# A real Fourier transform by matrix products: the second transform's features folded once more, into even and odd frequencies

## The chip, the cores and the metric

The kernel runs on one core of a Trainium2 chip. Its time is that of one execution on the device in microseconds. A core has five engines that take their own instructions in order and wait for each other by semaphores: TensorE (matrix products, with a weight load ahead of each), VectorE, ScalarE, GpSimd and SyncE; DMA queues move data beside them.

## The reference, cut to what matters

```python
# attention over 64-blocks (B=4, H=8, S=576, D=64), then x: (4, 576, 512)
x = x + relu(layernorm(x) * g_ln @ w_ch1) @ w_ch2            # first FFN, hidden 2048
X = np.fft.fft(x, axis=1)                                    # first transform: 576 tokens
X = np.fft.fft(X, axis=2)                                    # second transform: 512 features
u = x + np.real(X)
out = u + relu(layernorm(u) @ w2_ch1) @ w2_ch2               # second FFN
```

Only the real part of the two transforms is needed: cosines of tokens with cosines of features, less sines with sines.

## The kernel before, in words

The kernel goes through five stages that overlap: attention, first FFN, transform, second FFN and the preparation of weights for both. All products run on TensorE; precision beyond f16 is had by splitting each operand into a high and a low f16 part and adding three products (high-high, high-low, low-high), so each sum over 128 rows is three matmuls.

Tokens are kept in tiles by symmetry. For a batch b, X["E", b] holds 256 tokens and X["F", b] their mirror images; 64 tokens of each batch that are left over stand together in X["L"].

The transform of batch b has three steps.

- `dft_a1` (L1386) adds and subtracts E and F (xe, xo), which serves the token transform, and then `fold_rows` (L1337) adds feature f to feature 512 - f (for cosines over features) and subtracts it (for sines). The sums stand in places 1 to 255 and the differences in 257 to 511 of one row of 512, places 0 and 256 being features 0 and 256 themselves. Token 288 has a row of its own in one partition (g0). Then it scales by a power of two and splits into f16 parts: ge for the main tiles, gL for the left-over tokens, g0s for the one row; gL and g0s go by DMA from GpSimd's queue into a small tile gS.
- `dft_a2` (L1419) is the first matrix product (L1433), by features: five blocks (0, 1: cosines; 2, 3: sines; 4: the single feature 256), each with the token tables ct or sn, 289 columns. `dft_y` (L1438) copies and splits each result into y with ScalarE (L1440) and VectorE (L1441).
- `dft_b` (L1448) is the second matrix product, over features, from y: with the table cd (257 cosine columns, L1457; a single feature is added by two matmuls with the table row) and the table sd (255 sine columns, L1467). `dft_b_main` calls it for two row tiles of a batch, and once more without sines for the "pf" tile; `dft_b_left` calls it for the left-over tokens. `dft_apply` adds the result to E and F.

Beside this, `w_second` streams the second FFN's weights, in 32 pieces of one load each: ScalarE makes signs (L217), VectorE merges (L218), ScalarE squares and sums (L239). Pieces land in staging tiles (`w_stage`); the first 12 of them borrow buffers of the transform that are free until the transform starts, named by the list TAGS (L94) in rotation. The thirteenth and later ones use the two buffers wr.

What sets the order: `merge` gives each stream of work a planned time and takes the item with the earliest. A transform is six items of planned weight 10 (`dft_a1`), 1.2 each (`dft_a2`) and 2 (`dft_b_main`), between FFN products. Within this, instructions without a due partner may be placed ahead, by priority. TensorE then works strictly in that order.

Of the kernel before, what the change touches and what calls it, by code (L numbers as in the profile page):

```python
# [8 lines left out]
F32 = mybir.dt.float32  # L9
# [81 lines left out]
YE = 300  # L91
DV = (1, 0, 3)
R_F = 0.3
TAGS = ("wr", "wr", "xe", "xo", "ge", "y")  # L94
NT = 12
BLOCKS = ("B11", "B21", "B22", "T1", "T3", "T2", "T4")

# [2 lines left out]
def fused_kernel(ctx: ExitStack, tc: tile.TileContext, io: dict):  # L100
# [75 lines left out]
    def w_stage(n, name):  # L176
        shape = [128, n, 512, 4]
        if "pool" in wst:
            wst["k2"] = wst.get("k2", -1) + 1
            tag = TAGS[wst["k2"] % len(TAGS)] if wst["k2"] < NT else "wr"  # L180
            return wst["pool"].tile(shape, I16, tag=tag, bufs=WR if tag == "wr" else 1, name=name)
        wst["k"] = wst.get("k", -1) + 1
        if wst["k"] % 3 == 2 and wst["k"] < T3:
            return wpool.tile(shape, I16, tag="w", bufs=9, name=name)
        return a_tile(shape, I16, "stage", name)
# [1127 lines left out]
    def dft_setup(dctx):  # L1313
        wst["w1"] = ctx.enter_context(tc.tile_pool(name="w1pool", bufs=1))
        dp = dctx.enter_context(tc.tile_pool(name="dpool", bufs=1))
        D_["p"] = dp
        wst["pool"] = dp
        w_signs(dp, WN[1], NZ[1])
        for nm, shape in (
            ("ct", [128, 2, 2, 289]), ("sn", [128, 2, 2, 289]),  # L1320
            ("ctl", [98, 289]), ("snl", [96, 289]),
            ("cd", [128, 2, 2, 257]), ("sd", [128, 2, 2, 255]),
        ):
            t = dp.tile(shape, F16, name="c_" + nm)
            nc.gpsimd.dma_start(out=t, in_=io["c_" + nm])
            D_[nm] = t
        D_["row"] = dp.tile([128, 289], F16, name="c_row")
        nc.gpsimd.memset(D_["row"], 0.0)
        nc.gpsimd.dma_start(out=D_["row"][0:1, :], in_=io["c_row"])
        D_["yl"] = dp.tile([128, 4, 2, 128], F16, name="yl")  # L1330
        for nm, m, n in (("yl5", 2, 128), ("y5", 3, 289)):
            D_[nm] = dp.tile([128, m, n], F16, name=nm)
            nc.gpsimd.memset(D_[nm], 0.0)
        D_["invL"] = dp.tile([128, 1], F32, name="invL")
        D_["nL"] = dp.tile([128, 1], F32, name="nL")

    def fold_rows(a, d, out):  # L1337


        rev = slice(511, 256, -1)  # L1340
        nc.vector.tensor_tensor(
            out=out[..., 1:256], in0=a[..., 1:256], in1=a[..., rev], op=ALU.add
        )
        nc.vector.tensor_tensor(
            out=out[..., 257:512], in0=d[..., 1:256], in1=d[..., rev], op=ALU.subtract
        )

    def split(hi, lo, src, s):
        nc.scalar.activation(out=hi, in_=src, func=AF.Copy, scale=s)
# [11 lines left out]
    def dft_left_fold():  # L1361

        dp = D_["p"]
        xl = X["L"]
        sumsq(D_["nL"], [xl])
        xe, xo = (dp.tile([128, 2, DM], F32, tag=t, name=t) for t in ("xe", "xo"))
        a, d = xe[:, 0], xo[:, 0]
        nc.vector.tensor_tensor(out=a, in0=xl[:, 0], in1=xl[:, 1], op=ALU.add)
        nc.vector.tensor_tensor(out=d, in0=xl[:, 0], in1=xl[:, 1], op=ALU.subtract)
        fL = D_["fL"] = dp.tile([128, DM], F32, name="fL")  # L1370
        fold_rows(a, d, fL)
        nc.vector.tensor_copy(out=fL[:, 0:257:256], in_=a[:, 0:257:256])
        D_["gL"] = dp.tile([128, 2, DM], F16, name="gL")

    def dft_left_split(b, s):
        dp = D_["p"]
        q = slice(32 * b, 32 * b + 32)
        g = D_["gL"]
        split(g[q, 0], g[q, 1], D_["fL"][q], s[q, 0:1])
        st = dp.tile([98, DM], F16, tag="gS", bufs=GSB, name="gS")  # L1380
        nc.gpsimd.memset(st[96:98, 257:512], 0.0)
        for i, a in enumerate((0, 1, 0)):
            nc.gpsimd.dma_start(out=st[32 * i:32 * i + 32], in_=g[q, a])
        return st

    def dft_a1(b):  # L1386
        dp = D_["p"]
        E, F = X["E", b], X["F", b]
        n1 = sm.tile([128, 1], F32, tag="dn1", name="dn1")
        sumsq(n1, [E, F])  # L1390
        xe, xo = (dp.tile([128, 2, DM], F32, tag=t, name=t) for t in ("xe", "xo"))
        nc.vector.tensor_tensor(out=xe, in0=E, in1=F, op=ALU.add)
        nc.vector.tensor_tensor(out=xo, in0=E, in1=F, op=ALU.subtract)
        q = slice(32 * b, 32 * b + 32)
        nc.vector.tensor_tensor(out=n1[q], in0=n1[q], in1=D_["nL"][q], op=ALU.add)
        tot = all_sum(n1, 1, "dt")
        fold_rows(xe, xo, xe)
        r0, g0 = xo[0:1, 0], xo[0:1, 1, 0:257]
        nc.vector.tensor_tensor(
            out=g0[:, 1:256], in0=r0[:, 1:256], in1=r0[:, 511:256:-1], op=ALU.add  # L1400
        )
        nc.vector.tensor_copy(out=g0[:, 0:257:256], in_=r0[:, 0:257:256])
# [7 lines left out]
        g0s = dp.tile([1, 2, 257], F16, tag="g0s", name="g0s")  # L1410
        split(g0s[:, 0], g0s[:, 1], g0, s[0:1, 0:1])
        for a in range(2):
            nc.gpsimd.dma_start(out=st[96 + a:97 + a, 0:257], in_=g0s[:, a])
        g = dp.tile([128, 2, 2, DM], F16, tag="ge", name="ge")
        split(g[:, 0], g[:, 1], xe, s[:, 0:1])
        D_["g", b] = (g, st, s, inv)
        D_["y", b] = dp.tile([128, 4, 2, 289], F16, tag="y", name="y")

    def dft_a2(b, blk):  # L1419


        g, st, s, inv = D_["g", b]
        ev = blk in (0, 1, 4)
        f0, n = {0: (0, 128), 1: (128, 128), 2: (257, 128), 3: (385, 127), 4: (256, 128)}[blk]
# [20 lines left out]
        yl = D_["yl5"][0:1] if blk == 4 else D_["yl"][0:m, blk]  # L1445
        nc.gpsimd.tensor_copy(out=yl[:, :, 32 * b:32 * b + 32], in_=y[:, :, 256:288])

    def dft_b(yc, y5, ys, pool_bank):  # L1448

        mm = []  # L1450
        for a, w in ((0, 0), (0, 1), (1, 0)):
            for f in range(2):
                mm.append((yc(f, a), D_["cd"][:, f, w, :]))
        for a in range(2):
            mm.append((y5(a), D_["row"][:, 0:257]))
        for i, (l, r) in enumerate(mm):
            nc.tensor.matmul(  # L1457
                out=pool_bank[:, 0:257], lhsT=l, rhs=r, start=(i == 0), stop=(i == len(mm) - 1)
            )
        if ys is None:  # L1460
            return
        mm = []
        for a, w in ((0, 0), (0, 1), (1, 0)):
            mm.append((ys(0, a), D_["sd"][:, 0, w, :]))
            mm.append((ys(1, a), D_["sd"][0:127, 1, w, :]))
        for i, (l, r) in enumerate(mm):
            nc.tensor.matmul(  # L1467
                out=pool_bank[:, 257:512], lhsT=l, rhs=r, start=(i == 0), stop=(i == len(mm) - 1)
            )

    def dft_apply(pq, pf, inv, e, f):

# [207 lines left out]
def _hl(a):  # L1680
    a = np.asarray(a, np.float64) * CS
    hi = a.astype(np.float16)
    lo = (a - hi.astype(np.float64)).astype(np.float16)
    return np.stack([hi, lo])


def _consts():
# [13 lines left out]
    row = np.zeros((2, 289), np.float16)  # L1701
    row[:, 1::2] = CS
    c["ctl"] = np.concatenate([c["ctl"], row])
    f = np.arange(256)
    l = np.arange(257)
    cd = _hl(np.cos(2 * np.pi * ((f[:, None] * l[None, :]) % 512) / 512.0))
    c["cd"] = cd.reshape(2, 2, 128, 257).transpose(2, 1, 0, 3)
    f = np.arange(1, 257)
    l = np.arange(1, 256)
    sd = _hl(np.sin(2 * np.pi * ((f[:, None] * l[None, :]) % 512) / 512.0))  # L1710
    sd[:, 255] = 0
    c["sd"] = sd.reshape(2, 2, 128, 255).transpose(2, 1, 0, 3)
    row = np.zeros((1, 289), np.float16)
    row[0, 0:257] = CS * (1 - 2 * (np.arange(257) % 2))
# [65 lines left out]
```

## Time and profile before

| | |
|---|---|
| three runs | 994.78, 996.1, 999.83 us; median 996.1 |
| the profiled execution | 997.26 us, span 995.5 us |
| granted TensorE clock, mean over the span | 0.982 of full speed |
| TensorE busy | 946.1 us, 95% |
| VectorE busy | 673.7 us, 68% |
| ScalarE busy | 490.2 us, 49% |
| GpSimd busy | 72.5 us, 7% |

Busy times are sums over one profiled execution and an average over stages with different limits: a stage in which one engine is the limit can be one in which another is idle. The chain of waits is followed back from the last instruction, at each step to what released it. The ends of matmuls are modelled and overlap, so the pace of a series is read from their starts.

### The profile page before, as it was taken

The numbers are of one execution on the slowest core, as the hardware profiler recorded it, in microseconds if no ns is written. First come the engines' busy times: TensorE is split into PE (matmuls) and PEld (weight loads), VectorE is DVE, ScalarE is ACT, GpSimd is POOL, SyncE is SP. The second block draws the span as 40 slices with busy tenths as digits, with TensorE's granted clock in tenths as the row PEclk, the third lists the DMA queues.
The fourth block names the chain that finished last, engine by engine and source line by source line (L and its number), as shares of the span: only waits on it lengthen the run. The fifth ranks groups of instructions, "written<-read, shape, count | busy, mean of one in ns | idle before, by whom it ended". The sixth has DMA issues, their size and how long they took to land.

```text
span 995.5 us, 19447 instructions
## 1 busy us (share of the span) xinstructions
PE 946.1 (95%) x7758; PEld 700.8 (70%) x7758; DVE 673.7 (68%) x1677; ACT 490.2 (49%) x852; POOL 72.5 (7%) x184
## 2 busy tenths in 40 slices
PE   8898989998998999998999889999999999999998
PEld 6786654674674674766576665858588888888887
DVE  3886696665767666566587887669476776765754
ACT  5887664554554564426656654325153352342431
POOL 1000000002001010040011120100000000000000
PEclk9998999999999999999999989999999999999999
DMA  7657536758667666567408657011110111101100
GB/s 259 225 186 212 133 79 138 153 114 154 139 126 154 129 146 103 99 139 298 146 8 249 212 177 255 8 22 65 43 22 23 33 23 33 22 23 43 23 22 22
DMA packets 159195, 110.95 MB, mean 111 GB/s; under 512 B 134141, under 2 KB 141318, under 8 KB 157056
## 3 DMA queue, kind: packets, MB, share of 16 engines
q1 hardware_dynamic: 154640, 104.87, 40.8%
q0 software_dynamic: 2352, 4.32, 1.9%
q8 instruction: 61, 1.00, 0.4%
q10 hardware_dynamic: 2112, 0.52, 0.2%
q14 instruction: 30, 0.25, 0.1%
HBM read 64.19 MB, written 11.01 MB: 76 GB/s over the span
## 4 chain that ended last, share of the span: by engine, by line
PE 42%; DVE 7%; DMA 5%; ACT 3%; issue 1%; POOL 0%; ACTq 0%; POOLq 0%; DVEq 0%; SPq 0%
PE g L698 15%; PE s L748 13%; PE g L627 6%; PE g L679 4%; PE g L652 3%; DMA wr<-in_w 2%; DMA xnT1L<-xs 1%; ACT junk L239 1%; DVE ws L218 1%; DVE wq L339 1%; ACT sign L217 1%; DVE hT L637 1%; PE ya L1433 1%; DMA xnT2('F', 0)_7977<-xs 1%; DMA d<-ws 1%
## 5 line engine op out<-in xcount | busy, mean ns | idle before, releaser
L627 PEld LDWEIGHTS <-wq 128*128 128x128 f16 x2112 | 206.5, 99 | 47.9 <-issue 19.0
L652 PE MATMUL g<-wq,hT 128*128 128x512 f16 x768 | 184.2, 383 | 2.1 <-ACT hT L636 1.3
L698 PEld LDWEIGHTS <-wq 128*128 128x128 f16 x1344 | 131.5, 98 | 15.4
L652 PEld LDWEIGHTS <-hT 128*128 128x128 f16 x768 | 74.6, 99 | 90.2 <-issue 5.8
L748 PEld LDWEIGHTS <-hs 128*128 128x128 f16 x1176 | 115.1, 98 | 13.3
L715 ACT ACTIVATE hr<-g,tk 128x256 f32<-128x256 f32 x112 | 47.0, 470 | 143.1 <-PE g L698 143.1
L890 PE MATMUL pv<-vh,PT 128*128 128x65 f16 (+1 forms) x704 | 102.9, 203 | 14.6 <-DMA PT<-P 5.3
L919 DVE SCALAR_TENSOR_TENSOR P<-e,P 128x768 f16<-128x768 f32 (+2 forms) x56 | 54.6, 976 | 69.9 <-ACT P L918 69.8
L890 PEld LDWEIGHTS <-PT 128*128 128x128 f16 x1056 | 82.1, 101 | 28.1 <-issue 19.0
L723 DVE TENSOR_TENSOR hr<-hr 128x128 f32<-128x128 f32 x224 | 65.4, 292 | 48.3 <-ACT hr L715 40.4
L1167 ACT ACTIVATE e<-st,aq 128x384 f32<-128x384 f32 (+2 forms) x80 | 48.9, 652 | 91.3 <-DVE aq L1164 80.8
L748 PE MATMUL s<-tT,hs 128*128 128x256 f16 x672 | 75.7, 273 | 0.0
L637 DVE SCALAR_TENSOR_TENSOR hT<-g,hT 128x512 f16<-128x512 f32 x88 | 59.8, 683 | 19.3 <-ACT hT L636 19.1
L636 ACT ACTIVATE hT<-g 128x512 f16<-128x512 f32 x88 | 51.4, 588 | 34.2 <-PE g L627 34.1
L679 PE MATMUL g<-wq,hT 128*128 128x512 f16 x288 | 63.8, 379 | 0.2 <-DVE wq L339 0.2
L890 PE MATMUL pv<-vl,PT 128*128 128x64 f16 (+1 forms) x352 | 62.7, 203 | 0.0
L730 DVE TENSOR_TENSOR hs<-hr,hs 128x896 f16<-128x896 f32 x56 | 60.8, 1085 | 0.5
L748 PE MATMUL s<-tB,hs 128*128 128x256 f16 x504 | 57.3, 273 | 0.0
L218 DVE SCALAR_TENSOR_TENSOR ws<-wr,sign 128x512 int32<-128x512 int32 (+1 forms) x48 | 41.2, 863 | 23.2 <-ACT sign L217 20.6
L217 ACT ACTIVATE sign<-wr 128x512 f16<-128x512 bf16 (+1 forms) x48 | 46.5, 971 | 19.7 <-DMA wr<-in_w 19.0
L729 ACT ACTIVATE hs<-hr 128x896 f16<-128x896 f32 x56 | 53.1, 948 | 1.6 <-DVE hr L723 1.6
L679 PEld LDWEIGHTS <-hT 128*128 128x128 f16 x288 | 28.0, 98 | 32.4 <-issue 0.5
(425 smaller groups left out, 1516.4 us busy)
## 6 DMA issues: line engine op xcount, KB each, us to landing
wr<-in_w SPq DMA_DIRECT2D x16, 1023.5 KB, 6.0
wr<-in_w SPq DMA_DIRECT2D x32, 511.8 KB, 5.1
rawv<-in_vt SPq DMA_DIRECT2D x16, 320.0 KB, 2.9
k<-in_kt SPq DMA_DIRECT2D x16, 288.0 KB, 3.5
d<-ws SPq DMA_DIRECT2D x4, 1024.0 KB, 5.2
ws<-d SPq DMA_DIRECT2D x4, 1024.0 KB, 5.5
wt<-d SPq DMA_DIRECT2D x4, 1024.0 KB, 4.8
qz<-in_qt SPq DMA_DIRECT2D x32, 80.0 KB, 3.2
```

The lines of the kernel that those rows point to most:

```text
L217: nc.scalar.activation(out=z[:, :, :, 1], in_=r.bitcast(BF16)[:, :, :, 2], func=AF.Copy)
L627: nc.tensor.matmul(out=ps[:, i, :], lhsT=w1(ffn, k, wh, m), rhs=xt[:, xh, k, :], start=(n == 0), stop=(n == 3 * KT - 1),)
L637: nc.vector.scalar_tensor_tensor(out=h[:, :, 1, :], in0=ps, scalar=0.0, in1=h[:, :, 0, :], op0=ALU.max, op1=ALU.subtract,)
L652: nc.tensor.matmul(out=ps, lhsT=h[f // 4][:, f % 4, hh, t * 128:(t + 1) * 128], rhs=w2(ffn, f, wh), start=(f == 0 and hh == 0 and wh == 0) ...
L679: nc.tensor.matmul(out=g2["b"][t], lhsT=h[f // 4][:, f % 4, hh, t * 128:(t + 1) * 128], rhs=w2(ffn, f, wh), start=(f == 0 and hh == 0 and ...
L698: nc.tensor.matmul(out=ps[:, q, :], lhsT=w1(2, k, wh, i + 8 * q), rhs=xt[:, xh, k, :], start=(n == 0), stop=(n == 3 * KT - 1),)
L723: done = nc.vector.tensor_tensor(out=r[:, o], in0=r[:, a], in1=r[:, b], op=op)
L729: nc.scalar.activation(out=h[:, 0], in_=r[:, 1:8], func=AF.Copy)
L730: nc.vector.tensor_tensor(out=h[:, 1], in0=r[:, 1:8], in1=h[:, 0], op=ALU.subtract)
L748: nc.tensor.matmul(out=ps, lhsT=h[:, hh, hb], rhs=T[nm][:, wh, i], start=(i == 0 and hh == 0 and wh == 0), stop=(i == 7 and hh == 1),)
L890: nc.tensor.matmul(out=out[..., 0:w], lhsT=l, rhs=v[..., 0:w], start=(n == 0), stop=(n == len(mm) - 1))
L919: nc.vector.scalar_tensor_tensor(out=P[:, 1, 0:n], in0=e, scalar=PSC, in1=P[:, 0, 0:n], op0=ALU.mult, op1=ALU.subtract)
```

## The change

The features are folded a second time. After `fold_rows`, feature f and feature 256 - f are added and subtracted as well, for f up to 128. The sums give the even cosine frequencies and the odd sine frequencies, the differences the odd cosine and the even sine frequencies. Each block of 128 features then feeds half of the frequencies: the second product's four tables have 129, 128, 128 and 127 columns (ce, co, so, se) instead of two feature blocks with 257 and two with 255. The results are written into every second place of the output bank, so that it holds the frequencies in the same order as before.

The number of matmuls of `dft_b` stays the same. The first product keeps its number and shapes; only the places of the blocks move (block 2 to 256, block 4 to 384). The sums and differences of tokens, xe and xo, become one tile x2, and two staging tiles of the weights become its two halves (x2, x2b).

```diff
-TAGS = ("wr", "wr", "xe", "xo", "ge", "y")
+TAGS = ("wr", "wr", "x2", "x2b", "ge", "y")
...
+            if tag == "x2b":
+                return wst.pop("half")
+            if tag == "x2":
+                t = wst["pool"].tile([128, 2 * n, 512, 4], I16, tag=tag, name=name)
+                wst["half"] = t[:, n:]
+                return t[:, 0:n]
...
-            ("cd", [128, 2, 2, 257]), ("sd", [128, 2, 2, 255]),
+            ("ce", [128, 2, 129]), ("co", [128, 2, 128]),
+            ("so", [128, 2, 128]), ("se", [127, 2, 127]),
...
-    def fold_rows(a, d, out):
+    def fold_rows(x):
         rev = slice(511, 256, -1)
...
+        for eo, op in ((0, ALU.add), (1, ALU.subtract)):
+            nc.vector.tensor_tensor(
+                out=x[:, :, eo, 1:256], in0=x[:, :, eo, 1:256], in1=x[:, :, eo, rev], op=op
+            )
+
+    def fold_halves(x, sums, diffs):
+        for o, op in ((sums, ALU.add), (diffs, ALU.subtract)):
+            nc.vector.tensor_tensor(out=o, in0=x[..., 0:128], in1=x[..., 256:128:-1], op=op)
+
+    def fold_middle(x, o, e):
+        nc.vector.tensor_copy(out=o, in_=x[:, :, 1, 128:129])
+        nc.vector.tensor_copy(out=e, in_=x[:, :, 0, 128:129])
...
     def dft_left_fold():
...
+        x = dp.tile([128, 2, 2, DM], F32, tag="x2", name="x2")[:, 0:1]
+        for eo, op in ((0, ALU.add), (1, ALU.subtract)):
+            nc.vector.tensor_tensor(out=x[:, 0, eo], in0=xl[:, 0], in1=xl[:, 1], op=op)
+        fold_rows(x)
         fL = D_["fL"] = dp.tile([128, DM], F32, name="fL")
+        f2 = fL.rearrange("p (e f) -> p e f", e=2)
+        fold_halves(x[:, 0], f2[:, :, 0:128], f2[:, :, 128:256])
+        fold_middle(x, f2[:, 1:2, 0:1], f2[:, 1:2, 128:129])
...
     def dft_left_split(b, s):
...
-        nc.gpsimd.memset(st[96:98, 257:512], 0.0)
...
     def dft_a1(b):
...
+        x = dp.tile([128, 2, 2, DM], F32, tag="x2", name="x2")
+        for eo, op in ((0, ALU.add), (1, ALU.subtract)):
+            nc.vector.tensor_tensor(out=x[:, :, eo], in0=E, in1=F, op=op)
...
+        c0, g0 = (dp.tile([1, 257], F32, tag=t, name=t) for t in ("c0", "g0"))
         nc.vector.tensor_tensor(
+            out=c0[:, 1:256], in0=r0[:, 1:256], in1=r0[:, 511:256:-1], op=ALU.add
+        )
+        nc.vector.tensor_copy(out=c0[:, 0:257:256], in_=r0[:, 0:257:256])
+        fold_rows(x)
+        x4 = x.rearrange("p t e f -> p (t e) f")
+        fold_halves(x4, x4[..., 257:385], x4[..., 0:128])
+        fold_middle(x, x[:, :, 1, 257:258], x[:, :, 1, 0:1])
+        fold_halves(c0, g0[:, 0:128], g0[:, 128:256])
+        nc.vector.tensor_copy(out=g0[:, 256:257], in_=c0[:, 128:129])
...
-        split(g0s[:, 0], g0s[:, 1], g0, s[0:1, 0:1])
+        for a, c in ((0, 0), (1, 256)):
+            n = 256 - 255 * a
+            split(D_["g0s"][:, 0, c + 128 * a:c + 128 * a + n], D_["g0s"][:, 1, c + 128 * a:c + 128 * a + n],
+                  g0[:, c:c + n], s[0:1, 0:1])
         for a in range(2):
-            nc.gpsimd.dma_start(out=st[96 + a:97 + a, 0:257], in_=g0s[:, a])
+            nc.gpsimd.dma_start(out=st[96 + a:97 + a], in_=D_["g0s"][:, a])
...
-        split(g[:, 0], g[:, 1], xe, s[:, 0:1])
+        g4 = [g[:, a].rearrange("p t (e f) -> p (t e) f", e=2) for a in range(2)]
+        for c, o in ((257, 0), (0, 128)):
+            split(g4[0][..., o:o + 128], g4[1][..., o:o + 128], x4[..., c:c + 128], s[:, 0:1])
...
-    def dft_b(yc, y5, ys, pool_bank):
...
+    def dft_b(yc, y5, ys, bank):
+        passes = ((0, 0), (0, 1), (1, 0))
+        groups = [
+            (bank[:, 0:257:2], [(yc(0, a), D_["ce"][:, w]) for a, w in passes]
+             + [(y5(a), D_["row"][:, 0:129]) for a in range(2)]),
+            (bank[:, 1:256:2], [(yc(1, a), D_["co"][:, w]) for a, w in passes]),
+        ]
+        if ys is not None:
+            groups += [
+                (bank[:, 257:512:2], [(ys(0, a), D_["so"][:, w]) for a, w in passes]),
+                (bank[:, 258:511:2], [(ys(1, a), D_["se"][:, w]) for a, w in passes]),
+            ]
+        for out, mm in groups:
+            for i, (l, r) in enumerate(mm):
+                nc.tensor.matmul(out=out, lhsT=l, rhs=r, start=(i == 0), stop=(i == len(mm) - 1))
```

The constants of the host side follow (tables of 129, 128, 128 and 127 columns).

## Rows read from the trace of the kernel before

**Rows 1.** The page, busy time of each engine, with share and instructions.

```profile
PE 946.1 (95%) x7758; PEld 700.8 (70%) x7758; DVE 673.7 (68%) x1677; ACT 490.2 (49%) x852; POOL 72.5 (7%) x184
```

**Rows 2.** Stretches: us, busy PE, PEld, DVE, ACT, POOL; PE clock, DMA share, GB/s.

```profile
503.00:525.00 22.00, 22.00 (x199) 19.23 (x198) 21.15 (x52) 13.83 (x27) 4.65 (x9) 1.00 0.13 40
...
550.00:578.00 28.00, 20.48 (x160) 15.54 (x158) 23.01 (x71) 17.27 (x38) 5.90 (x13) 0.94 0.63 218
578.00:600.00 22.00, 22.00 (x156) 15.96 (x155) 18.00 (x55) 8.81 (x17) 2.67 (x7) 0.92 0.54 173
600.00:664.00 64.00, 63.06 (x457) 44.66 (x455) 46.71 (x110) 22.71 (x43) 7.27 (x20) 1.00 0.30 97
664.00:996.00 332.00, 327.82 (x2863) 279.77 (x2860) 217.15 (x482) 125.48 (x211) 0.00 (x0) 1.00 0.11 30
```

**Rows 3.** TensorE's waits, 495 to 720 us: total, times, longest.

```profile
PE pq L1467 <- ACT y L1440: 6.0, 3, 4.7
```

**Rows 4.** The chain of waits, 495 to 720 us: start us, us, what.

```profile
503.59 0.76 DVE XxL L664
...
514.95 1.20 DVE xo L1393
516.15 1.20 DVE ge L1350
...
520.60 0.61 DVE ws L218
...
567.03 0.59 DVE xe L1344
567.62 0.11 DVE xo L1402
...
568.35 5.46 DMA wr<-in_w
...
577.75 1.25 PE pq L1467 x5
579.00 1.72 PE pf L1457 x8
...
618.21 0.88 PE pq L1457 x8
619.09 0.67 PE pq L1467 x6
```

**Rows 5.** Line L1457: ns minimum/median/maximum, first and last start, forms.

```profile
L1457 PE MATMUL pq<-c_cd,y x48: 270/273/274, 531.3 to 656.8; 128*128 128x257 f16 x48
```

**Rows 6.** TensorE in order of time, attention: first and last of six rows.

```profile
317.71 0.22 PE L890 MATMUL pv<-vh,PT 128*128 128x130 f16 x1 [4.02 <-DVE aq L1164]
...
318.00 0.38 PE L652 MATMUL g<-wq,hT 128*128 128x512 f16 x1
```

**Rows 7.** VectorE and ScalarE by form, 500 to 660 us: busy us, mean ns, idle.

```profile
L637 DVE SCALAR_TENSOR_TENSOR hT<-g,hT 128x512 f16<-128x512 f32 x24 | 16.3, 682 | 8.1 <-ACT hT L636 8.1
...
L1350 DVE SCALAR_TENSOR_TENSOR ge<-xe,dsc,ge 128x1024 f16<-128x1024 f32 x4 | 5.1, 1274 | 0.7 <-ACT ge L1349 0.6
...
L1341 DVE TENSOR_TENSOR xe<-xe 128x510 f32<-128x510 f32 x4 | 2.7, 674 | 0.0
...
L1399 DVE TENSOR_TENSOR xo<-xo 1x255 f32<-1x255 f32 x4 | 1.7, 414 | 0.0
...
L1402 DVE COPY xo<-xo 1x2 f32<-1x2 f32 x4 | 0.6, 160 | 0.0
...
L1349 ACT ACTIVATE g0s<-xo,dsc 1x257 f16<-1x257 f32 x4 | 2.0, 508 | 0.1
```

**Rows 8.** VectorE's last table and TensorE's first use, in order of time.

```profile
697.70 1.27 DVE L446 SCALAR_TENSOR_TENSOR tT<-wt,tk,tT 128x1024 f16<-128x1024 f32 x1
...
737.51 5.40 PE L748 MATMUL s<-tB,hs 128*128 128x256 f16 x48
```

**Rows 9.** Line L1433, columns as in rows 5.

```profile
L1433 PE MATMUL ya<-c_ct,ge x72: 284/287/288, 519.1 to 642.7; 128*128 128x289 f16 x72
```

More of the change, by code (lines that the diff above doesn't have):

```diff
@@ L1333, in dft_setup @@
             nc.gpsimd.memset(D_[nm], 0.0)
+        D_["g0s"] = dp.tile([1, 2, DM], F16, name="g0s")
+        nc.gpsimd.memset(D_["g0s"], 0.0)
         D_["invL"] = dp.tile([128, 1], F32, name="invL")
         D_["nL"] = dp.tile([128, 1], F32, name="nL")
-    def fold_rows(a, d, out):
+    def fold_rows(x):
         rev = slice(511, 256, -1)
[L1341 to L1346, printed above, removed]
+        for eo, op in ((0, ALU.add), (1, ALU.subtract)):
[8 more added lines that the diff above has]
+        nc.vector.tensor_copy(out=e, in_=x[:, :, 0, 128:129])
     def split(hi, lo, src, s):
@@ L1365, in dft_left_fold @@
         sumsq(D_["nL"], [xl])
[L1366 to L1369, printed above, removed]
+        x = dp.tile([128, 2, 2, DM], F32, tag="x2", name="x2")[:, 0:1]
+        for eo, op in ((0, ALU.add), (1, ALU.subtract)):
+            nc.vector.tensor_tensor(out=x[:, 0, eo], in0=xl[:, 0], in1=xl[:, 1], op=op)
+        fold_rows(x)
         fL = D_["fL"] = dp.tile([128, DM], F32, name="fL")
-        fold_rows(a, d, fL)
-        nc.vector.tensor_copy(out=fL[:, 0:257:256], in_=a[:, 0:257:256])
+        f2 = fL.rearrange("p (e f) -> p e f", e=2)
+        fold_halves(x[:, 0], f2[:, :, 0:128], f2[:, :, 128:256])
+        fold_middle(x, f2[:, 1:2, 0:1], f2[:, 1:2, 128:129])
         D_["gL"] = dp.tile([128, 2, DM], F16, name="gL")
@@ L1390, in dft_a1 @@
         sumsq(n1, [E, F])
-        xe, xo = (dp.tile([128, 2, DM], F32, tag=t, name=t) for t in ("xe", "xo"))
-        nc.vector.tensor_tensor(out=xe, in0=E, in1=F, op=ALU.add)
-        nc.vector.tensor_tensor(out=xo, in0=E, in1=F, op=ALU.subtract)
+        x = dp.tile([128, 2, 2, DM], F32, tag="x2", name="x2")
+        for eo, op in ((0, ALU.add), (1, ALU.subtract)):
+            nc.vector.tensor_tensor(out=x[:, :, eo], in0=E, in1=F, op=op)
         q = slice(32 * b, 32 * b + 32)
@@ L1396, in dft_a1 @@
         tot = all_sum(n1, 1, "dt")
-        fold_rows(xe, xo, xe)
-        r0, g0 = xo[0:1, 0], xo[0:1, 1, 0:257]
+        r0 = x[0:1, 0, 1]
+        c0, g0 = (dp.tile([1, 257], F32, tag=t, name=t) for t in ("c0", "g0"))
         nc.vector.tensor_tensor(
-            out=g0[:, 1:256], in0=r0[:, 1:256], in1=r0[:, 511:256:-1], op=ALU.add
+            out=c0[:, 1:256], in0=r0[:, 1:256], in1=r0[:, 511:256:-1], op=ALU.add
         )
-        nc.vector.tensor_copy(out=g0[:, 0:257:256], in_=r0[:, 0:257:256])
+        nc.vector.tensor_copy(out=c0[:, 0:257:256], in_=r0[:, 0:257:256])
[5 more added lines that the diff above has]
+        nc.vector.tensor_copy(out=g0[:, 256:257], in_=c0[:, 128:129])
         s = pow2_scale(tot, 1, 10, f"dsc{b}")
@@ L1409, in dft_a1 @@
         st = dft_left_split(b, s)
-        g0s = dp.tile([1, 2, 257], F16, tag="g0s", name="g0s")
-        split(g0s[:, 0], g0s[:, 1], g0, s[0:1, 0:1])
+        for a, c in ((0, 0), (1, 256)):
+            n = 256 - 255 * a
+            split(D_["g0s"][:, 0, c + 128 * a:c + 128 * a + n], D_["g0s"][:, 1, c + 128 * a:c + 128 * a + n],
+                  g0[:, c:c + n], s[0:1, 0:1])
         for a in range(2):
-            nc.gpsimd.dma_start(out=st[96 + a:97 + a, 0:257], in_=g0s[:, a])
+            nc.gpsimd.dma_start(out=st[96 + a:97 + a], in_=D_["g0s"][:, a])
         g = dp.tile([128, 2, 2, DM], F16, tag="ge", name="ge")
-        split(g[:, 0], g[:, 1], xe, s[:, 0:1])
+        g4 = [g[:, a].rearrange("p t (e f) -> p (t e) f", e=2) for a in range(2)]
+        for c, o in ((257, 0), (0, 128)):
+            split(g4[0][..., o:o + 128], g4[1][..., o:o + 128], x4[..., c:c + 128], s[:, 0:1])
         D_["g", b] = (g, st, s, inv)
@@ L1423, in dft_a2 @@
         ev = blk in (0, 1, 4)
-        f0, n = {0: (0, 128), 1: (128, 128), 2: (257, 128), 3: (385, 127), 4: (256, 128)}[blk]
+        f0, n = {0: (0, 128), 1: (128, 128), 2: (256, 128), 3: (385, 127), 4: (384, 128)}[blk]
         m = 1 if blk == 4 else n
@@ L1446, in dft_y @@
         nc.gpsimd.tensor_copy(out=yl[:, :, 32 * b:32 * b + 32], in_=y[:, :, 256:288])
-    def dft_b(yc, y5, ys, pool_bank):
[L1450 to L1469, printed above, removed]
+    def dft_b(yc, y5, ys, bank):
[13 more added lines that the diff above has]
+                nc.tensor.matmul(out=out, lhsT=l, rhs=r, start=(i == 0), stop=(i == len(mm) - 1))
     def dft_apply(pq, pf, inv, e, f):
@@ L1703, in _consts @@
     c["ctl"] = np.concatenate([c["ctl"], row])
[L1704 to L1712, printed above, removed]
+    f = np.arange(128)
+    turn = lambda fn, f, l: _hl(fn(2 * np.pi * ((f[:, None] * l[None, :]) % 512) / 512.0))
+    odd = np.arange(1, 256, 2)
+    c["ce"] = turn(np.cos, f, np.arange(0, 257, 2)).transpose(1, 0, 2)
+    c["co"] = turn(np.cos, f, odd).transpose(1, 0, 2)
+    c["so"] = turn(np.sin, np.where(f == 0, 128, f), odd).transpose(1, 0, 2)
+    c["se"] = turn(np.sin, f[1:], np.arange(2, 255, 2)).transpose(1, 0, 2)
     row = np.zeros((1, 289), np.float16)
-    row[0, 0:257] = CS * (1 - 2 * (np.arange(257) % 2))
+    row[0, 0:129] = CS * (1 - 2 * (np.arange(129) % 2))
     c["row"] = row
```

## The prediction

> **What bounds the kernel now.** I read the shares of the engines first, then the busy time by stretch, then the waits of TensorE, then the chain of waits, and last the single instructions of the second transform. The reader is to see in the shares that TensorE is busy for 95% of the span [rows 1], and in the stretches that this holds to the end: from 664 us on it is busy for 327.82 of 332 us, and from 600 to 664 us for 63.06 of 64 [rows 2]. What is taken from TensorE after about 578 us should therefore come off the end, if nothing else becomes late. The one hole near the change is from 550 to 578 us: busy 20.48 of 28, so 7.5 us idle. The waits say on what: the second matrix product of the second transform (L1467) waits 6.0 us in all for ScalarE's copy of the first product, y (L1440), 4.7 of them at once [rows 3]. The chain says why that copy is late. From 503.59 to 521.21 us the chain is VectorE almost without a gap, then it alternates between VectorE's decoding of weights (L218), the loads that this decoding sets free (5.46 us for one of them) and ScalarE, until TensorE is released at 577.75 us [rows 4]. From there to the end nearly all of it is TensorE's. So I call 577.75 us the gate: before it VectorE's order of work counts, after it TensorE's work counts. VectorE is busy for 21.15 of 22 us in the first part of that stretch [rows 2].
>
> **What the change does to TensorE.** The second product (dft_b) has 14 matmuls for each of nine row tiles (eight of the four batches, one for the left-over tokens) and 8 for each of four "pf" tiles: 9 x 14 + 4 x 8 = 158, in both versions. Before, each streams 257 or 255 columns; after, 129, 128 or 127. Their pace before is 0.88 us for 8 and 0.67 us for 6 in the chain [rows 4], 111 ns each, 17.5 us in all; the single durations of 273 ns [rows 5] overlap and are no pace. The matmuls of the first product (L1433) keep number and shape.
>
> What a matmul of the new shape costs isn't in the trace, because every output there lies word beside word in its bank, and the new ones write every second word (0:257:2, 1:256:2 and so on). The ends are these. By columns, the nearest row is the attention product with 128 to 130 columns and its own weight load for each matmul: five start between 317.71 and 318.00 us, so 58 ns [rows 6]; 158 of them take 9.2 us, and 8.3 us are saved. By the stretch of the bank that is passed over, the nearest row is the old product itself: 127 to 129 words with a gap between them reach over the same 253 to 257 words, 111 ns, and nothing is saved. I take the second, though not by much: the columns are half as many, but the words written lie over the old extent, and no row shows a spread output at the pace of a dense one. Both ends stay in the range.
>
> On the lower end the Trainium skill (TensorE: Matmul & The Clock Gate, section Back-to-back issue gap) speaks against the row: it gives about 81 ns for a sustained stream of weight load and 128-column matmul. The trace shows 58 ns, so the measurement decides; by the page the most that could be saved, as an estimate, would be 158 x 30 ns = 4.7 us. On the spread output itself the Trainium skill (PSUM — Partial Sum Buffer, section Specifications) says that a pattern that isn't contiguous slows matmuls significantly, without a figure; no row of this kernel shows one.
>
> **What the change adds on VectorE.** Per batch: two sums and differences of f with 256 - f over four blocks of 128 (512 elements each); the nearest row is L1341 with 510 elements, 674 ns [rows 7], of which the chain shows 0.59 as the step to the next instruction (L1344 [rows 4]), so 1.2 us. Two copies of the middle element, two elements per partition, like L1402 with 160 ns [rows 7] and a step of 0.11 [rows 4]: 0.2. Two half-length folds of the one-partition row, each half of the 414 ns of L1399: 0.4. One copy and one more split of a single element, again by L1402: 0.2. The large split in two halves of 512 (682 ns each by L637 against 1274 whole): 0.1 [rows 7]. Sum 2.1 us. For the left-over tokens, two folds of 256 elements, half of 0.59 each, and two copies: 0.8 us. In all 4 x 2.1 + 0.8 = 9.2 us. ScalarE gets two more instructions per batch, each below the 508 ns of the one-row split [rows 7]; it is idle for a third and more of the stretch [rows 2], so only their place ahead of a y copy could cost. GpSimd loses four memsets; its transfers of the extra row grow from 257 to 512 numbers and stay off the chain. The transform's constants take half the bytes.
>
> How much of it lies on the path? The left-over fold and batch 0 (0.8 + 2.1) fall where the chain is VectorE alone, 503.59 to 521.21 us: all 2.9 us count. Batch 1's folds and copies come where the chain mostly waits for transfers and need not delay it: 0 to 1.3. Batch 2's folds stand in the chain at 567.03 us, just ahead of the decoding that starts the last long load [rows 4]: 0 to 2.1. Batch 3's come after the gate, in a stretch in which TensorE has other work throughout [rows 2]: 0. The upper end is 2.9 + 1.3 + 2.1 = 6.3 us. Below zero: the two buffers of sums and differences become one, so batch 1's difference (1.20 us at 514.95 in the chain [rows 4]) can't be put ahead of batch 0's split any more, and if it lands in a hole of VectorE the chain is shorter by 1.2. I take the certain part, 2.9.
>
> Merging the buffers also pairs two weight stages: the second use of that buffer waits for both decodings instead of one. The decodings that this touches come before the transform starts, and four other stages hold loads meanwhile; I cost it at nothing. If that cover failed, one load would come late by at most its own length, 5.46 us by the row [rows 4].
>
> The wait at risk: TensorE takes its work in order. Behind L1467, which waits for y, stand pf, the next tile and the following FFN products; they all move with the gate. Behind the gate nothing else becomes late: the last table of the second FFN is written at 698.97 us and TensorE first reads one at 737.51 [rows 8], so 38 us of cover.
>
> **Sum.** The profiled execution took 997.26 us (span 995.5), 1.2 above the median of the runs shown, 996.1. With TensorE unchanged and 2.9 us more ahead of the gate: 997.26 + 2.9 = 1000.2, and 1.2 less against the median, 999.0; I forecast 999 us, which is no change: about 0.5% (5 us) is what a measurement of this kernel can tell from none. The forecast's own range is 996.1 - 1.2 = 995 to 996.1 + 6.3 = 1002.
>
> **Rivals.**
> 1. *Spread outputs run at the dense pace.* For: five narrow matmuls with their own weights at 58 ns [rows 6]. Against: their outputs are dense. Behind the gate batch 1 has 27 matmuls left: 1.25 + 1.72 us and a tile of 0.88 + 0.67 us now [rows 4], of which 13 run at half clock; at 58 ns and twice that for those 13 they take 2.3 us, so 2.2 are saved. Batch 2: 36 x 53 ns = 1.9. Batch 3: 1.9, less 0.4 because its wait for y grows when TensorE comes sooner: 1.5. Left-over: 14 x 53 ns = 0.75. Together 6.35 us; batch 0's 1.9 us fall ahead of the gate and only lengthen the idle 7.5. 999.0 - 6.35 = 992.6 us; with the chain's bounds, 988.5 to 996.
> 2. *Slower: VectorE's additions all reach the gate and TensorE's clock falls once more.* Place: batch 0's split ends at 516.15 + 1.20 = 517.35 us [rows 4] and TensorE takes it up at 519.1 [rows 9], 1.75 us of cover; 2.9 us more opens a hole there, and the hole before the gate, after which TensorE runs at half clock (granted 0.92 in 578 to 600 us [rows 2]), gets longer. It decides from the point where more than those 1.75 us land ahead of batch 0's split. Price: 6.3 us plus the same half-clock loss again, 13 matmuls in 1.25 + 1.72 us instead of 13 x 111 ns, 1.5 us: 996.1 + 7.8 = 1003.9. Against: TensorE has other matmuls ahead in the order.
> 3. *Spread outputs cost more than their extent.* If each took twice 111 ns, the 113 matmuls after the gate add 12.5 us: 1011.5 us. Nothing in the trace speaks for it; only the absence of such a row leaves it open.
> That the change doesn't do what it says, fewer columns at the same sums, I exclude: the diff halves them.
>
> **How the numbers follow.** Forecast 0.40, rival 1 0.35, rival 2 0.18, rival 3 0.07. Faster by over 0.5% (below 991.1) holds about half of rival 1 and a seventh of the forecast: 0.24. Slower by over 0.5% (above 1001.1): rival 3, nearly all of rival 2 and a tenth of the forecast: 0.27. Within: 0.49. The range 988.5 to 1005 takes in rival 1 nearly whole, the forecast, and rival 2 at its price; rival 3 and the far ends are left out.
>
> **What would show it.** In the changed kernel's trace, the starts of the narrow matmuls of one group: 107 to 111 ns apart (forecast), 58 (rival 1), over 200 (rival 3). VectorE's new folds at about 0.6 us each, four times two, and the release of the last product of batch 1 later than 577.75 us by 2 to 4 us. If the narrow matmuls stand at 58 ns and the gate hasn't moved, I am wrong on both terms. If the planned order of the engines shifts elsewhere, the stretch after 664 us will differ from 332 us, and the sum doesn't hold.

## The result and the profile after

The changed kernel takes 989.08 us (median of ten runs, 983.98 to 995.03) against 995.92 us for the kernel before (ten runs). The ratio is 0.9914, 95% interval 0.9891 to 0.9936: 0.86% faster. (This ratio and those below come from the single runs with their scatter; they are not quotients of the medians, which here would give 0.69%.) The forecast was no change, 999 us. The measured time lies in the stated range, near rival 1's price, but rival 1's mechanism is not what happened: that the range holds it is luck. The profiled execution took 989.96 us, span 988.2. Among the ten runs time goes with the granted clock: the shortest, 983.98 us, has a mean of 0.991, the longest, 995.03, of 0.978. The two profiled executions have 0.982 before and 0.981 after, so a higher clock over the whole span is not what divides them.

The page of the changed kernel, engines' busy time, answers to [rows 1]:

```profile
PE 947.6 (96%) x7758; PEld 704.1 (71%) x7758; DVE 681.1 (69%) x1716; ACT 491.8 (50%) x860; POOL 72.4 (7%) x183
```

TensorE is not relieved at all (946.1 before), and VectorE has 7.4 us more. The gain is therefore not in any engine's busy time. The stretches, to be laid beside [rows 2], say where it is:

```profile
503.00:525.00 22.00, 21.97 (x199) 19.18 (x198) 21.93 (x58) 14.13 (x29) 4.54 (x9) 1.00 0.02 6
...
550.00:578.00 28.00, 24.85 (x206) 20.12 (x205) 24.85 (x68) 19.66 (x43) 8.76 (x17) 1.00 0.70 253
578.00:600.00 22.00, 22.00 (x147) 14.23 (x146) 21.61 (x63) 13.59 (x25) 0.58 (x3) 1.00 0.69 219
600.00:664.00 64.00, 63.45 (x455) 45.48 (x454) 46.98 (x117) 21.61 (x39) 6.75 (x20) 1.00 0.23 76
```

From 550 to 578 us TensorE is busy 24.85 us instead of 20.48, and its granted clock is 1.00 in this stretch and the next, instead of 0.94 and 0.92. TensorE's waits from 495 to 720 us [rows 3] (total, times, longest):

```profile
PE pq L1492 <- ACT y L1469: 3.7, 3, 2.7
PE pq L1492 <- DVE y L1470: 0.4, 1, 0.4
```

The 6.0 us for ScalarE's y became 3.7. The chain of waits of the changed kernel [rows 4] shows what releases the gate now (line numbers differ from kernel to kernel: L1492 here is `dft_b`, L1467 and L1457 before):

```profile
502.56 0.76 DVE XxL L670
...
563.73 7.14 DMA wr<-in_w
570.89 0.79 ACT sign L223
571.71 0.69 DVE ws L224
...
572.83 0.65 PE pq L1492 x4
573.47 0.88 PE pf L1492 x8
574.35 2.62 PE g L633 x24
576.97 1.53 PE pq L1492 x14
578.50 7.86 PE g L633 x72
```

The gate stands at 572.83 us, where it stood at 577.75. The 14 narrow matmuls of a row tile take 1.53 us, 109 ns each (1.55 us before). And behind the gate the group of eight pf matmuls takes 0.88 us and the FFN group of 24 takes 2.62, at full clock, where they took 1.72 and 3.01. The chain before had, behind the pf group:

```profile
580.72 3.01 PE g L627 x24
...
585.28 7.86 PE g L627 x72
```

Why the gate moved is read from ScalarE's instructions in order of time (start, us, line, shape; in brackets the idle time before it and its releaser). First the kernel before:

```profile
570.98 0.77 ACT L217 ACTIVATE sign<-wr 128x512 f16<-128x512 bf16 x1
573.83 0.77 ACT L217 ACTIVATE sign<-wr 128x512 f16<-128x512 bf16 x1 [2.08 <-DMA wr<-in_w]
574.63 0.72 ACT L1349 ACTIVATE gL<-fL,dsc 32x512 f16<-32x512 f32 x1
575.37 0.60 ACT L636 ACTIVATE hT<-g 128x512 f16<-128x512 f32 x1
575.99 0.51 ACT L1349 ACTIVATE g0s<-xo,dsc 1x257 f16<-1x257 f32 x1
576.40 0.39 ACT L1440 ACTIVATE y<-ya 128x289 f16<-128x289 f32 x1
```

and the changed kernel:

```profile
570.89 0.78 ACT L223 ACTIVATE sign<-wr 128x512 f16<-128x512 bf16 x1 [0.55 <-DMA wr<-in_w]
571.54 0.69 ACT L1469 ACTIVATE y<-ya 128x289 f16<-128x289 f32 x2
...
573.06 0.77 ACT L223 ACTIVATE sign<-wr 128x512 f16<-128x512 bf16 x1
573.85 0.72 ACT L1368 ACTIVATE gL<-fL,dsc 32x512 f16<-32x512 f32 x1
```

The last sign, at 573.83 us before and at 577.87 after, is that of the 32nd and last piece. In the kernel before, all 32 pieces and batch 2's gL and g0s stand ahead of batch 1's last two y copies, so these copies wait for the last weight load, which they don't need. What they do need had long been there; TensorE's last matmuls of the two first products, in the kernel before:

```profile
566.85 0.29 PE L1433 MATMUL ya<-c_snl,gS 96*128 96x289 f16 x1
567.82 0.29 PE L1433 MATMUL ya<-c_snl,gS 96*127 96x289 f16 x1
```

After the change 30 pieces stand ahead of the two copies; signs 31 and 32 and batch 2's split stand behind. The copies still wait, for the 30th load.

### The profile page after: what moved, and what is told of

It reads as the page before. It is cut to its first block, busy times and chain, and to the rows that moved or that the text cites. A ratio compares the mean times of both kernels' runs of the same rounds, so it can differ in the third digit from the quotient of the medians.

```text
span 988.2 us, 19494 instructions
## 1 busy us (share of the span) xinstructions
PE 947.6 (96%) x7758; PEld 704.1 (71%) x7758; DVE 681.1 (69%) x1716; ACT 491.8 (50%) x860; POOL 72.4 (7%) x183
## 4 chain that ended last, share of the span: by engine, by line
PE 43%; DVE 6%; DMA 4%; ACT 3%; issue 1%; POOL 0%; SPq 0%; ACTq 0%; DVEq 0%; POOLq 0%
PE g L704 15%; PE s L754 13%; PE g L633 6%; DMA wr<-in_w 4%; PE g L685 4%; PE g L658 3%; DVE wq L345 1%; ACT junk L245 1%; ACT sign L223 1%; PE pq L1492 1%; PE ya L1462 1%; DVE hT L643 1%; DMA xnT2('F', 0)_8023<-xs 1%; DVE ws L224 1%; DVE x L1412 0%
```

## The experiments

The profiles of different kernels begin the transform at different times: the left-over tokens' last sum, XxL, starts between 495.64 and 503.59 us, and differs also where an edit touches only what comes later (501.14 us in e6, 495.64 in e7). So positions are told from that start; the times themselves are medians, and each ratio is to the kernel before as run beside that experiment. "Gate" is where TensorE goes on after its last wait in the sine product of batch 1's first row tile.

| kernel | median us | ratio to before, 95% | gate − start | span − start |
|---|---|---|---|---|
| before | 995.92 | | 74.16 | 491.9 |
| changed | 989.08 | 0.9914 [0.9891, 0.9936] | 70.27 | 485.6 |
| e1_pieces_behind | 990.32 | 0.9937 [0.9909, 0.9964] | 69.42 | 485.5 |
| e2_merge_only | 993.49 | 0.9972 [0.9948, 0.9996] | 72.46 | 488.0 |
| e3_folds_only | 997.01 | 1.0014 [0.9993, 1.0034] | 74.69 | 492.0 |
| e4_dense_outputs | 986.83 | 0.9898 [0.9871, 0.9926] | 69.82 | 483.5 |
| e5_after_behind | 983.95 | 0.9888 [0.9864, 0.9911] | 66.33 | 483.0 |
| e6_dense_right | 983.08 | 0.9874 [0.9846, 0.9901] | 71.03 | 485.4 |
| e7_dense_behind | 982.49 | 0.9883 [0.9852, 0.9913] | 64.55 | 483.1 |
| e9_two_behind | 993.50 | 0.9960 [0.9944, 0.9976] | 73.53 | 491.6 |
| e10_two_and_split_behind | 990.81 | 0.9949 [0.9928, 0.9969] | 71.00 | 488.3 |
| e11_dense_four_behind | 985.04 | 0.9899 [0.9874, 0.9923] | 66.14 | 482.0 |

(The changed kernel by the same subtraction: 572.83 − 502.56 and 988.2 − 502.56. For e6 the profiled execution, 988.26 us, is the longest of its six runs.)

**The order alone, in the kernel before.** e1 puts the last four pieces behind batch 1's last y copies (`issue_after` gives an instruction its place in the queue behind another):

```diff
+LATE = ((2, 3, 0), (2, 3, 1), (2, 3, 2), (2, 3, 3))
...
-            w_decode(2, which, c, i, n)
+            with ExitStack() as behind:
+                if (which, c, i) in LATE:
+                    for got in D_["copied", 1, 3]:      # the last y copies of batch 1
+                        behind.enter_context(tc.issue_after(got.ins))
+                w_decode(2, which, c, i, n)
```

> The kernel before, with one change of order: the last four weight pieces (their sign on ScalarE, their merge on VectorE) stand behind batch 1's last y copy instead of ahead of it, so 28 of 32 pieces stand ahead of y and not 32. No arithmetic and no buffer is changed. Theory (order of the queues): TensorE's release at the last product of batch 1 comes 5 us or more earlier than 577.75, TensorE does not fall to half clock there, and the time is 0.6 to 1.0% shorter than before, all of what the change gained. Rival (the merged buffer or the new folds give the gain): within 0.2% of before. Rival (narrower matmuls give it): within 0.2% of before.

Measured: 0.63% faster with not one instruction computed otherwise, at the lower end of what the theory expected and outside both rivals. The y wait shrank from 6.0 us to 0.8. One of the other waits stayed, for VectorE's half of y, and the half clock came there instead. TensorE in order of time:

```profile
562.39 1.02 PE L1438 MATMUL ya<-c_sn,ge 128*128 128x289 f16 x6 [2.03 <-DVE y L1446]
...
563.45 1.66 PE L1438 MATMUL ya<-c_sn,ge 128*127 128x289 f16 x6
```

Six matmuls that took 1.02 us take 1.66 in the next group (granted clock 0.94 from 550 to 578 us). That wait, 1.9 us in the kernel before too, is gone in the changed one.

e9 and e10 go closer to the changed kernel's own order: `LATE = ((2, 3, 2), (2, 3, 3))`, so that 30 pieces stand ahead, and in e10 batch 2's split (gL, g0s) stands behind as well:

```diff
+        with ExitStack() as behind:
+            if b == 2:
+                for got in D_["copied", 1, 3]:
+                    behind.enter_context(tc.issue_after(got.ins))
             st = dft_left_split(b, s)
...
```

> The kernel before, nothing computed otherwise; only the last two weight pieces stand behind batch 1's last y copies in ScalarE's and VectorE's queues (30 of 32 ahead, as in the changed kernel; batch 2's gL still stands ahead, as in the kernel before). Theory (the place of the last two pieces carries the change's gain): ScalarE no longer waits 2.08 us for the next-to-last load ahead of y, the gate moves from 577.75 to 573 to 575, and the time is 990 to 993, a ratio of 0.994 to 0.997. Rival (the gain comes from the changed transform itself, the order being of no account): 995 to 997, a ratio of 0.999 to 1.001.

> As e9_two_behind, and batch 2's split (gL and g0s of ScalarE, with VectorE's halves of it) stands behind batch 1's last y copies too: the order of the changed kernel with the arithmetic of the one before. Theory: the whole of the change's gain but for what the start of the transform gave (1.0 us of 7.3): 989 to 992, a ratio of 0.993 to 0.996, the gate at 572 to 574. Rival (the changed transform itself carries it): 995 to 997.

Measured: 0.40% and 0.51% faster, both ratios inside what the order theory expected and their intervals outside the rival's (e9's median is 0.5 us above its expected range). e10 has nearly the order of the changed kernel and the arithmetic of the one before, and its ratio 0.9949 is some six tenths of the whole gain; in its profile 3.7 of 6.3 us (span less start, 491.9 to 488.3 against 485.6). One difference of order shows: batch 2's large split, ge, stands between the two y copies on ScalarE, where the changed kernel has it behind both.

```profile
568.88 0.39 ACT L1449 ACTIVATE y<-ya 128x289 f16<-128x289 f32 x1
569.37 1.15 ACT L1354 ACTIVATE ge<-xe,dsc 128x1024 f16<-128x1024 f32 x1
570.43 0.39 ACT L1449 ACTIVATE y<-ya 127x289 f16<-127x289 f32 x1
```

In e9 the time came but the profile shows only 0.4 us of it (491.9 to 491.6), so what e9 gained is not shown by its trace. What e10 lacks stands behind its waits, TensorE in order of time:

```profile
570.88 0.62 PE L1477 MATMUL pq<-c_sd,y 127*128 127x255 f16 x4 [1.23 <-ACT y L1449]
572.55 0.28 PE L1477 MATMUL pq<-c_sd,y 127*128 127x255 f16 x1 [1.05 <-DVE y L1450]
...
573.63 4.37 PE L632 MATMUL g<-xnT1('F', 3)_6721,wq 128*128 128x256 f16 x24
```

The FFN group behind them took 4.37 us; the same group by the same view takes 2.83 in the changed kernel, whose clock stays whole: 1.5 of the missing 2.6 us.

**Parts of the change alone.** e2 merges xe and xo (and the two staging tiles) and changes nothing else; e3 leaves the buffers and adds the VectorE work, two folds of 512 elements per batch that nothing reads:

```diff
+        x2 = dp.tile([128, 2, 2, DM], F32, tag="x2", name="x2")
+        xe, xo = x2[:, 0], x2[:, 1]                          # e2
...
+        for op in (ALU.add, ALU.subtract):                   # e3
+            nc.vector.tensor_tensor(out=xo[:, 0, :], in0=xe[:, 0, :], in1=xe[:, 1, :], op=op)
```

> The kernel before with the merged buffer alone (sums and differences of tokens in one tile, two weight stages as its halves); folds, tables and products as before. Theory (order): what counts is the number of pieces ahead of batch 1's last y on ScalarE, 31 here against 32 before and 30 in the changed kernel, so a gain of 1 to 3 us at most. Rival (merged buffer is the cause): 0.9% faster, as the changed kernel.

> The kernel before with two more VectorE folds of 512 elements per batch on data that nothing reads (the size of the added folds); everything else as before. Theory (order): 31 pieces ahead of y and not 32, a gain of 0 to 3 us although VectorE does 5 us more. The prediction's step (added VectorE work delays the gate): 2 to 3 us slower than before. Rival (merged buffer): no gain, slower by up to 3 us.

Measured: the merge alone gives 0.28%, as the order theory expected and not the 0.9% of its rival; the folds alone give 0.14% more time with an interval from 0.7 us faster to 3.4 us slower. In each the planner puts 31 pieces ahead of the last y copy, one less than before. The gate of e3, and the pf group behind it, in order of time:

```profile
576.72 0.40 PE L1469 MATMUL pq<-c_sd,y 127*128 127x255 f16 x1 [0.46 <-DVE y L1443]
576.91 1.50 PE L1459 MATMUL pf<-c_cd,y 128*128 128x257 f16 x6
```

Counted from the transform's start its gate is 0.5 us later than before (74.69 against 74.16), not 2.9. But one piece has moved behind as well, which by itself makes the gate earlier, and the interval of the time reaches the 2 to 3 us of the prediction's step. So e3 does not show what the added VectorE work costs under an unchanged order.

**The price of the spread outputs.** e4 writes the four results side by side instead of into every second word. It leaves out the order of the frequencies: results go to the wrong places.

```diff
-            (bank[:, 1:256:2], [(yc(1, a), D_["co"][:, w]) for a, w in passes]),
+            (bank[:, 129:257], [(yc(1, a), D_["co"][:, w]) for a, w in passes]),
...
-                (bank[:, 257:512:2], [(ys(0, a), D_["so"][:, w]) for a, w in passes]),
+                (bank[:, 257:385], [(ys(0, a), D_["so"][:, w]) for a, w in passes]),
```

> The changed kernel with the four results of the second product side by side in the bank instead of in every second place; what reads the bank is left as it is, so frequencies land in wrong places (left out: their order). Same columns, same number of matmuls. If the gap between the written words sets the pace: 55 to 58 ns from matmul to matmul against 109, and 113 x 0.053 = 6 us less after the gate, so 0.5 to 0.7% faster than the changed kernel, some 1.4% faster than before. If the pace is set by something else (weight load, short matmuls): 109 ns stays or 81 ns, and the time is that of the changed kernel, 0.9% faster than before, or 0.3% below it.

The chain of e4:

```profile
571.18 0.66 PE pq L1492 x4
571.83 0.87 PE pf L1492 x8
572.70 4.63 PE g L633 x24
577.33 0.80 PE pq L1492 x14
```

At full clock 14 matmuls take 0.80 us, 57 ns each instead of 109, as expected if the gap sets the pace. But the time fell by only 0.2 points against the changed kernel and not by 0.5 to 0.7, with intervals that overlap: in this kernel the clock fell behind the y wait (granted 0.88 from 550 to 578 us), and the FFN group took 4.63 us instead of 2.62.

e6 is the same with the results read back in order by two ScalarE copies and two-dimensional views on VectorE, so that nothing is left out:

```diff
-        nc.scalar.activation(out=qc[:, 1:256], in_=pq[:, 257:512], func=AF.Copy, scale=inv)
+        nc.scalar.activation(out=qc[:, 1:256:2], in_=pq[:, 257:385], func=AF.Copy, scale=inv)
+        nc.scalar.activation(out=qc[:, 2:255:2], in_=pq[:, 385:512], func=AF.Copy, scale=inv)
...
+            cos = p[r, 0:258].rearrange("p (e i) -> p i e", e=2)[:, 0:128]
```

> The changed kernel with dense results of the second product, read back into the order of frequencies by ScalarE (two copies instead of one) and VectorE (reads that jump between the two blocks, and one more small instruction per use). Output complete. Theory (gap sets the pace, order sets the gate): matmuls at 57 ns; the gate stays where the loads put it, TensorE arrives there earlier, idles longer and may run at half clock behind it again, so of 6 us only 1 to 3 come off: 1.0 to 1.2% below before. Rival (TensorE's own work is all that counts): 1.5% below before.

Measured: 983.08 us, 1.26% below before; against the changed kernel the intervals overlap (0.9846 to 0.9901 and 0.9891 to 0.9936). The interval holds the 1.0 to 1.2% of the theory and the 1.5% of its rival, so the time does not decide between them. Its clock, too, was 0.88 from 550 to 578 us.

e8 asks which outputs are slow. In each batch's second row tile it adds 36 matmuls of 128 columns in six groups of six (the expectation says three, and so counts 72 matmuls in all where there are 144): dense, every third word, every fourth word, pairs of neighbours that begin at an even word, pairs that begin at an odd word, every second word.

> The changed kernel with six more groups of three 128-column matmuls ahead of the real ones in each second row tile, which write the same bank in different patterns and are overwritten: side by side, every third word, every fourth word, two words of every four from an even place, the same from an odd place, every second word. If each access takes an aligned pair of words: 57 ns side by side and for pairs from an even place, 109 ns for every second, third and fourth word and for pairs from an odd place. If the extent counts: 57, 160, 213, 109, 109, 109 ns. 72 more matmuls make it 4 to 8 us slower than the changed kernel.

The series of batch 0 in order of time:

```profile
533.57 3.45 PE L1498 MATMUL pq<-c_co,y 128*128 128x128 f16 x36
536.82 0.54 PE L1498 MATMUL pq<-c_ce,y 128*128 128x129 f16 x3
```

The 36 take 536.82 − 533.57 = 3.25 us. With dense and even pairs at 55 ns and the other four groups at 109, the sum is 12 x 55 + 24 x 109 = 3.28 us; if only the dense group were fast it would be 3.6, if both kinds of pairs were 3.0, if each cost its extent (the expectation's second row of paces) 4.5. The starts of the single matmuls in the trace agree: from one to the next it is 55 to 57 ns in the dense group, 108 to 110 with every third and every fourth word, 55 to 56 with pairs from an even word, 108 to 110 with pairs from an odd word and with every second word, and the same to within 2 ns in the three other batches. So a word costs by pairs that begin at an even word: a pair half used costs as much as one fully used, and the extent costs nothing (every fourth word, over 509 words, is no slower than every second). The one run of e8 took 1001.07 us, 12 above the changed kernel's median where 4 to 8 were expected; four series of 3.25 us are 13.

**How much more the order can give.** e5 is the changed kernel with its last five pieces behind the y copies; e7 and e11 are e6 with the last five and the last four behind (the same edit as e1).

> The changed kernel with its last five weight pieces behind batch 1's last y copy (27 of 32 ahead of y instead of 30). Theory (order): the wait of 2.7 us for y at the last product of batch 1 goes or falls below 1 us, the gate comes at 569 to 571 us, and the time is 0.2 to 0.4% below the changed kernel's, 1.1 to 1.3% below before. Rival (the loads themselves arrive earlier in the changed kernel, whatever the order): no change against the changed kernel.

> The kernel of dense, reordered results, with the last five weight pieces behind batch 1's last y copy as well. Theory: with the wait gone TensorE's saving is no longer eaten ahead of the gate: no half clock, 1.5 to 1.9% below before, the best of all. Rival: the two gains are the same one, 1.2%.

> As e7_dense_behind, but only the last four pieces stand behind batch 1's y copies instead of five. Theory (the fifth piece's decode, pushed into batch 3's time, made batch 3's wait for its split on ScalarE, 3.1 us, and the half clock behind it): that wait shrinks below 1 us, TensorE stays at full clock from 600 to 664, and the time is 977 to 981, a ratio of 0.982 to 0.985. Rival (batch 3's wait comes from the shorter matmuls, whatever stands behind): the wait stays over 2 us and the time is 981 to 984, a ratio of 0.986 to 0.989.

Measured, e5: 983.95 us, 1.12% below before, inside what the theory expected; the intervals of e5 and of the changed kernel overlap, so that the time alone does not exclude the rival. The gate came at 564.34 us, ahead of the 569 to 571 expected, in an execution whose transform began 4.6 us earlier than the changed kernel's. The stretch of the gate has no hole left:

```profile
550.00:578.00 28.00, 28.00 (x254) 25.19 (x252) 25.59 (x67) 17.34 (x39) 4.34 (x9) 1.00 0.64 234
```

e7 has 57 ns matmuls and hardly a hole there, and should have added the two gains (1.5 to 1.9%). It reached 1.17%, the number of its rival (1.2%). In batch 3 a wait stands that the changed kernel doesn't have, and the half clock behind it; TensorE of e7 in order of time:

```profile
618.88 0.67 PE L1467 MATMUL ya<-c_ct,ge 128*128 128x289 f16 x4 [3.13 <-ACT ge L1373]
620.26 0.66 PE L1467 MATMUL ya<-c_ct,ge 128*128 128x289 f16 x2 [0.72 <-DVE ge L1374]
621.54 0.40 PE L1467 MATMUL ya<-c_ctl,gS 98*128 98x289 f16 x1 [0.62 <-DMA gS<-g0s]
621.74 5.09 PE L638 MATMUL g<-xnT2('E', 0)_7592,wq 128*128 128x256 f16 x24
```

and the same place in e11, with one piece less behind:

```profile
624.67 0.67 PE L1467 MATMUL ya<-c_ct,ge 128*128 128x289 f16 x4 [1.44 <-ACT ge L1373]
626.05 0.42 PE L1467 MATMUL ya<-c_ct,ge 128*128 128x289 f16 x2 [0.72 <-DVE ge L1374]
627.33 0.28 PE L1467 MATMUL ya<-c_ctl,gS 98*128 98x289 f16 x1 [0.85 <-DMA gS<-g0s]
627.45 2.78 PE L638 MATMUL g<-xnT2('E', 0)_7592,wq 128*128 128x256 f16 x24
```

The first wait fell from 3.1 to 1.4 us, not below the 1 us that the theory named, and the clock stayed whole; but the wait for VectorE's half of y grew (2.3 us where e7 has 0.4; for ScalarE's half 1.9 and 1.8), and the time, 985.04 us, is no better: a ratio of 0.990, outside what the theory expected and what its rival did. In e7 and e11 the hole has moved: what TensorE no longer does, or no longer waits for at the gate, it waits for at the next thing that ScalarE and VectorE deliver. Of the versions run, e5, e6 and e7 are 1.1 to 1.3% below before; their intervals don't tell them apart.

## Why the prediction was wrong, step by step

- **TensorE's work unchanged: right.** 109 ns was measured for a matmul of half the columns, 111 before; busy time 947.6 against 946.1 us. The reason given ("the words written lie over the old extent") was wrong, so the right number is luck: e8 shows no price on extent, but one on half-used pairs, and it doubles the cost of half the columns. Rival 1's pace, 58 ns, needs dense outputs: e4 shows 57.
- **VectorE's added work, 9.2 us: a little high.** It is 7.4 us more in all.
- **"The certain part, 2.9 us" ahead of the gate: wrong, and this is the step that failed**, with its consequence that the last product of batch 1 is released "later than 577.75 us by 2 to 4 us". It was released 4.9 us earlier, 3.9 counted from the transform's start. Two things are in it. The work ahead of batch 0's split was covered: that split ends at 517.87 us (a row below), 1.55 later than before when counted from the transform's start, yet TensorE stayed busy for 21.97 of 22 us. And the path from VectorE to the gate was taken as fixed. The weight pieces did come later: the 30th sign at 570.89 instead of 565.96 us, and the 32nd load, issued at 572.43 and 3.7 us on its way, lands at 576.1 instead of 573.8 (its sign, at 577.87, waits for other work of ScalarE and no longer for the load). But the planner now puts the y copies behind the 30th piece instead of the 32nd. Had the order stayed, the gate would have come some 2.3 us later than before (an estimate from the two landings; that kernel was not run), which lies in the "2 to 4 us" of the prediction. So what failed in that step is that it priced added work in an order of the queues that it took as given. The chain's row of the split in the changed kernel [rows 4]:

```profile
516.55 1.32 DVE ge L1369 x2
```

- **Behind the gate: what was not forecast is the clock.** From the gate to the group of 72 FFN products it took 585.28 − 577.75 = 7.53 us before, 578.50 − 572.83 = 5.67 after. The matmuls are no faster; before, 13 of the second product and part of the FFN group ran at half clock [rows 2, 4], after, none. So 3.9 us of order, 1.9 of clock and 1.0 of an earlier start make 6.8 of the 7.3 us between the two profiled executions. The other 0.5 lies between there and the group of 192 FFN products at 675.04 and 667.71 us in the chains, from which both kernels need 320.5 us to the end. That 1.0 can't be told from the scatter of the start among kernels that differ only in what comes later.
- **Rival 2 named the right places, but they did not turn slower.** The split and the gate were the places to watch; the 1.75 us of cover at batch 0's split held, with 0.2 left (the split ends at 517.87 us, TensorE takes it up at 518.08).
- **The last sentence of the prediction** ("if the planned order of the engines shifts elsewhere") named the mechanism but gave it neither a price nor a chance, and its sign does not show it: the stretch after 664 us is shorter, 324 us for 332, only because all that comes before it ends earlier. That there was something to gain could have been read: at the gate [rows 3, 4] y waited behind a load of 5.46 us that has nothing to do with it.

What stays open: which part of the change makes the planner's order (merge alone and folds alone each move one piece, all together two and the split); how the changed transform would run in the old order; what makes up the four tenths of the gain that e10 lacks, beyond 1.5 us of clock and the place of ge; why the clock did not fall in the changed kernel but did in e10, e4 and e6; and what makes the start of the transform vary by up to 8 us among the profiles.

## What to carry to other kernels

Read the chain not only for what is late, but for what stands ahead of it in the same queue without being needed: there reordering alone, with no work saved, gave 0.4 to 0.6% here (e1, e9, e10). When a change alters buffers or adds work in a kernel whose order is planned, price the order itself: list, for the engine at the gate, which of its queued instructions could stand behind. Before halving the columns of a matmul, look at the output's pattern: here 128 f32 words cost 109 ns when every second word is written and 57 when they are dense.

## What the runs showed of the hardware

Matmuls with 128 columns and their own weights stand 57 ns apart when the f32 output is dense and 109 ns when it takes every second word (e4, changed kernel); every third and fourth word cost the same as every second, pairs that begin at an odd word too, and pairs that begin at an even word as much as dense (55 to 57 ns; e8). The Trainium skill (PSUM — Partial Sum Buffer, section Specifications) gives cachelines of 8 bytes, two f32 words, and says that any pattern that isn't contiguous slows matmuls; the traces agree with the pair of words, but a pattern of whole pairs, which isn't contiguous either, ran at the dense pace.

The granted clock does not follow from the length of a single wait: it stayed whole after waits of 2.71 and 0.45 us in the changed kernel, and was at the lower of its two levels after 2.03 us in e1 and after 1.23 and 1.05 us in e10 (the FFN group of 24 in 4.37 us instead of 2.83). What tells these apart no run here shows.
